# Channel attention with a squared-ReLU feed-forward: the sums of the squares' blocks on GpSimd, and both roundings one step later

## The chip, the cores and the metric

The kernel runs on one core of one Trainium2 chip. The metric is the device time of one execution in microseconds, as a median over runs. The core's engines work in parallel, each through its own instructions in order: TensorE (PE in the profile; PEld are its weight loads) multiplies matrices, ScalarE (ACT) and VectorE (DVE) work elementwise, GpSimd (POOL) too, and SyncE (SP) issues the transfers. They wait for one another through semaphores.

## The reference

```python
# q, k, v: (4, 6080, 256), tau: scalar; w_in: (256, 2048), w_out: (2048, 256), all fp32
qn = q / (norm(q, axis=1) + 1e-6); kn = k / (norm(k, axis=1) + 1e-6)
s = kn.transpose(0, 2, 1) @ qn / tau            # 256 x 256 for each batch
a = softmax(s)
x = (v @ a).reshape(4 * 6080, 256)
h = maximum(x @ w_in, 0)
out = (h * h) @ w_out
```

## The kernel before

**Two products.** The attention matrix of a batch is multiplied into w_in once, to W (256 x 2048), so that for each block of tokens only two products are left: the first, v by W, then ReLU and square, and the second, by w_out. A batch has 12 blocks of tokens, 10 of 512 columns and 2 of 480, in all 48 blocks. fp32 accuracy comes from splitting each operand in a rounded part (`hi`) and a remainder (`lo`) and adding three products: hi by hi, hi by lo, lo by hi.

**Steps.** The loop over `i` at the end of the kernel (line 964) goes through the steps; a step is one of the 16 feature tiles (128 features) of a block. `part` is 0 in an even and 1 in an odd step. Two steps make a pair `(b, n, r)`, 8 pairs make a block. In each step `first_product` (line 712) issues 6 matmuls of 512 columns into PSUM (`ps_h`, 3 buffers) and one eviction with ReLU by ScalarE into half of the pair's tile `x`. The tile has 8 slots of 256 columns; slots 0 to 3 are the four plain blocks (two feature tiles by two halves of the tokens). It lies in a pool with two buffers for this tag.

**Seven products in place of eight.** From the third block on, `by_seven` (line 704) is true, up to the first 5 pairs of the last block: 365 pairs. The second product of a pair is then a 2 x 2 block product done with seven block products (the Strassen-Winograd form): on the side of the squares it needs the plain blocks 1, 2 and 3 and four sums of blocks, in slots 4 to 7. `squares_and_sums` (line 736), in the odd step, has ScalarE square slots 0 to 3, VectorE make the four sums (one subtraction of two slots, one addition, one subtraction), ScalarE round the three plain blocks to `g_hi` (a CAST of 768 columns) and VectorE make their remainder `g_lo`. `parts_of_sums` (line 749), in the next even step, rounds the four sums (1024 columns) and makes their remainder; it is the last reader of `x`. `g_hi` and `g_lo` have two buffers each. The first two blocks use `eight_products`, without sums.

**Order of the work.** Every engine's instructions keep the order in which the program issues them (`InProgramOrder`, line 19). The second product of a pair (`second_product`, line 762) comes two pairs later (`LAG = 2`): in the even step `seven_products` uses plain blocks 1 to 3 (9 matmuls of 256 columns into `ps_o`), in the odd step the four sums (12 matmuls). At the end of a block ScalarE copies the 3 and 4 accumulated blocks to `o`, after the even and the odd part, and `combine` (line 822) adds them up on VectorE, piece by piece in later odd steps, and has SP write them out.

**Work beside it.** While the blocks of one batch run, a generator (`attention`, line 433) issues the attention of the next one piece by piece: in an even step, between the eviction and the work on the pair, one piece of ScalarE and VectorE (in turn the rounding of a chunk of q and k with its remainder, and its squares with their addition), and matmuls into `gram`. Two steps of each block go without. Afterwards the same generator makes the softmax and W. `split_v_hi` and `split_v_lo` round the next block's v at steps 6 and 8 of a block.

Of the kernel before, what the change touches and what calls it, by code (L numbers as in the profile page):

```python
# [30 lines left out]
def kernel(  # L31
# [22 lines left out]
    tensor, vector, scalar, pool_engine = (  # L54
        InProgramOrder(tc, e) for e in (nc.tensor, nc.vector, nc.scalar, nc.gpsimd)
    )
# [624 lines left out]
    def load_v(b, n, tag="v"):  # L681
        t0, tn = blocks[n]
        raw = pool.tile([P, NC, T], F32, tag=tag, name=f"v{b}_{n}", bufs=1)
        nc.sync.dma_start(raw[:, :, :tn], vT[b, :, t0 : t0 + tn].rearrange("(c p) t -> p c t", p=P))
        V[b, n] = [raw, None, None]

    def split_v_hi(b, n):
        tn = blocks[n][1]
        V[b, n][1] = pool.tile([P, NC, T], F32R, tag="v_hi", name=f"v_hi{b}_{n}")
        scalar.copy(V[b, n][1][:, :, :tn], V[b, n][0][:, :, :tn])  # L690
# [5 lines left out]
    def split_v_lo(b, n):  # L696
        tn = blocks[n][1]
        raw, hi, _ = V[b, n]
        V[b, n][2] = pool.tile([P, NC, T], F32R, tag="v_lo", name=f"v_lo{b}_{n}")
        vector.tensor_sub(V[b, n][2][:, :, :tn], raw[:, :, :tn], hi[:, :, :tn].bitcast(F32))  # L700
# [3 lines left out]
    def by_seven(b, n, r):  # L704


        return (0, 1) < (b, n) and ((b, n) != order[-1] or r < SWITCH)

    X = {}
    G = {}  # L710

    def first_product(b, n, f):
        tn = blocks[n][1]
        _, v_hi, v_lo = V[b, n]
        w_hi, w_lo = W[b, f // FPG]
        f0 = (f % FPG) * P
        ps = ps_h.tile([P, T], F32, tag="h", name=f"ps_h{b}_{n}_{f}")
        parts = [(c, x, y) for x, y in ((w_hi, v_hi), (w_hi, v_lo), (w_lo, v_hi)) for c in range(NC)]
        for i, (c, wt, vt) in enumerate(parts):
            tensor.matmul(  # L720
                ps[:, :tn], wt[:, c, f0 : f0 + P], vt[:, c, :tn], start=i == 0, stop=i == len(parts) - 1
            )
        if f % 2 == 0:
            X[b, n, f // 2] = pool.tile([P, 8, tn // 2], F32, tag="x", name=f"x{b}_{n}_{f // 2}")
        x = X[b, n, f // 2].rearrange("p s t -> p (s t)")
        s = slice((f % 2) * tn, (f % 2 + 1) * tn)
        scalar.activation(x[:, s], ps[:, :tn], AF.Relu)
# [3 lines left out]
    def parts_of(b, n, r):  # L731
        half = blocks[n][1] // 2
        shape = [P, 7 if by_seven(b, n, r) else 4, half]
        return [pool.tile(shape, F32R, tag=name, name=f"{name}{b}_{n}_{r}") for name in ("g_hi", "g_lo")]

    def squares_and_sums(b, n, r):

        x = X[b, n, r]
        G[b, n, r] = hi, lo = parts_of(b, n, r)
        scalar.activation(x[:, 0:4, :], x[:, 0:4, :], AF.Square)  # L740
        if by_seven(b, n, r):
            hi_, lo_, src = hi[:, 0:3, :], lo[:, 0:3, :], x[:, 1:4, :]
            vector.tensor_sub(x[:, 4:6, :], x[:, 1:3, :], x[:, 0:1, :].broadcast_to(list(x[:, 1:3, :].shape)))
            scalar.copy(hi_, src)
            vector.tensor_add(x[:, 6, :], x[:, 2, :], x[:, 4, :])
            vector.tensor_sub(x[:, 7, :], x[:, 3, :], x[:, 6, :])
            vector.tensor_sub(lo_, src, hi_.bitcast(F32))

    def parts_of_sums(b, n, r):

        x = X.pop((b, n, r))
        hi, lo = G[b, n, r]
        if by_seven(b, n, r):
            hi, lo, src = hi[:, 3:7, :], lo[:, 3:7, :], x[:, 4:8, :]
        else:
            src = x[:, 0:4, :]
        scalar.copy(hi, src)
        vector.tensor_sub(lo, src, hi.bitcast(F32))
# [3 lines left out]
    def second_product(b, n, r, part):  # L762
        if by_seven(b, n, r):
            seven_products(b, n, r, part)
        elif (b, n) == order[-1]:
            final_products(b, n, r, part)
        else:
            eight_products(b, n, r, part)
# [145 lines left out]
    pairs = [(b, n, f // 2) for b, n, f in steps[::2]]  # L914
# [49 lines left out]
    for i in range(len(steps) + 2 * LAG):  # L964
        part = now["part"] = i % 2
        if i < len(steps):
            b, n, f = steps[i]
            at = b * NB + n
            first_product(b, n, f)
            if n == NB - 1 and f % FPG == FPG - 1:  # L970
                may_write_W.add((b + 1, f // FPG))

        if i >= PAIR:
            gens = (beside,)
        else:
            if i == 1:
                split_v_lo(*order[1])
            for item in stages.get(i, ()):
                weights.stage(item)
            gens = (first,) if i in steps_of_W else ()  # L980
            if i >= 16 and (i >= 24 or part == 0):
                gens += (squares_of_heads if B > 1 and grams[1].raws else sums,)

        if i >= PAIR and steps[min(i, len(steps) - 1)][2] in (2 * LAG - 2, 2 * LAG - 1):
            gens = ()
        if i < PAIR or part == 0:
            for gen in gens:
                next(gen, None)
        if part == 0 and 0 <= i // 2 - 1 < len(pairs):
            parts_of_sums(*pairs[i // 2 - 1])  # L990
        if part == 1 and i // 2 < len(pairs):
            squares_and_sums(*pairs[i // 2])
        if (part or i >= len(steps)) and late_work:
            if next(late_work[0], "end") == "end":
                late_work.pop(0)
        if i == 2 * LAG:
            for _ in heads:
                pass
        if i >= 2 * LAG:
            second_product(*pairs[i // 2 - LAG], part)  # L1000
        if i in steps_of_W:
            next(first)
        if i < len(steps):
            at_hi, at_lo = (None, None) if at == 0 else (12, 13) if at == 1 else (6, 8)
            if i == 2 and len(order) > 2:
                load_v(*order[2])
            if f == at_hi and at + 1 < len(order):
                split_v_hi(*order[at + 1])
            if f == at_lo and at + 1 < len(order):
                split_v_lo(*order[at + 1])  # L1010
                if at + 2 < len(order):
                    load_v(*order[at + 2])
        if i >= PAIR and part:
            for gen in gens:
                next(gen, None)
# [27 lines left out]
```

## Time and profile before

| | |
|---|---|
| median of 2 runs | 2214.74 us (2213.72 to 2215.77) |
| span of the profiled execution | 2211.6 us |
| busy: TensorE, weight loads | 2203.1 us, 1985.0 us |
| busy: VectorE | 1818.0 us, 2614 instructions |
| busy: ScalarE | 1859.1 us, 2347 instructions |
| busy: GpSimd | 0.7 us, 6 instructions |

The times are those of the runs without a profile; the profiled execution's own time is its span, from the first to the last instruction. In the profile's groups all lines are that of a helper (L27), so instructions are told apart by their tiles and sizes: ACT `x<-ps_h` is the eviction, ACT `x<-x` the square, ACT `g_hi<-x` of 768 and 1024 columns the rounding of the plain blocks and of the sums, DVE `g_lo<-x,g_hi` the remainders, DVE `x<-x` the four sums. Pairs of the last two blocks of a batch have 480, 720, 960 and 240 where the others have 512, 768, 1024 and 256. In a row of a timeline the first number is the start and the second the duration, both in us; in brackets stands the engine's idle time before it and what ended it. In a row of windows the busy time and the number of instructions of PE, PEld, DVE, ACT and POOL follow on the window's length, then the granted TensorE clock, the DMA share and GB/s.

### The profile page before, as it was taken

To read this page: it belongs to the slowest core of one execution; us is meant where nothing else is said; L and a number is where in the kernel's file an instruction comes from. 1 tells how busy PE (TensorE), PEld (TensorE's weight loads), DVE (VectorE), ACT (ScalarE), POOL (GpSimd) and SP (SyncE) were. 2 spreads that over 40 slices of the span, in tenths; PEclk is the share of its full clock that TensorE was granted. 3 is DMA by queue.
4 is the path that set the end of the run, shared out by engine and by line. 5 is a ranking of instruction groups with operands and counts; after the bars stand their busy time and mean duration, and the time that the engine had idled before them with its cause. 6 is when DMAs were issued, how large, how long until landed. Compare 5 with 4: busy or idle time off the path is not lost.

```text
span 2211.6 us, 34981 instructions
## 1 busy us (share of the span) xinstructions
PE 2203.1 (100%) x13903; PEld 1985.0 (90%) x13903; DVE 1818.0 (82%) x2614; ACT 1859.1 (84%) x2347; POOL 0.7 (0%) x6
## 2 busy tenths in 40 slices
PE   9999999999999999999999999999999999999999
PEld 8789999988999999998999999999899988888898
DVE  6878888889888888878888888887888877787776
ACT  5788888888888888888878888888888888888887
POOL 0000000000000000000000000000000000000000
PEclk9999999999999999999999999999999999999999
DMA  9521122023421122210122122111103010010000
GB/s 342 179 77 39 61 77 65 27 76 109 157 86 58 60 62 71 63 60 21 36 95 86 60 66 76 58 53 60 33 24 115 22 36 20 22 37 20 20 28 19
DMA packets 82261, 148.03 MB, mean 67 GB/s; under 512 B 8368, under 2 KB 35760, under 8 KB 82096
## 3 DMA queue, kind: packets, MB, share of 16 engines
q1 hardware_dynamic: 82096, 145.79, 19.9%
q8 instruction: 109, 1.79, 0.3%
q14 instruction: 56, 0.46, 0.1%
HBM read 112.46 MB, written 33.29 MB: 66 GB/s over the span
## 4 chain that ended last, share of the span: by engine, by line
PE 92%; DVE 3%; DMA 2%; ACT 2%; issue 0%; SPq 0%; DVEq 0%; ACTq 0%
PE ps_h L27 46%; PE ps_o L27 41%; PE gram L27 4%; PE ps_w L27 2%; DMA qk<-in_k 1%; DVE g_lo L27 1%; DVE x L27 1%; ACT x L27 1%; DMA qk<-in_q 0%; DMA qk_heads<-in_q 0%; ACT g_hi L27 0%; DVE o L27 0%; DMA w_raw<-in_w_in 0%; DVE dec_m L27 0%; DMA wi_lo<-wi_kept 0%
## 5 line engine op out<-in xcount | busy, mean ns | idle before, releaser
L27 DVE TENSOR_TENSOR g_lo<-x,g_hi 128x768 fp32r<-128x768 f32 (+2 forms) x749 | 808.2, 1079 | 71.7 <-ACT g_hi L27 71.1
L27 DVE TENSOR_TENSOR x<-x 128x512 f32<-128x512 f32 (+1 forms) x1095 | 558.2, 510 | 244.0 <-ACT x L27 218.3
L27 ACT CAST g_hi<-x 128x768 fp32r<-128x768 f32 (+2 forms) x749 | 702.1, 937 | 42.8 <-DVE x L27 30.0
L27 ACT ACTIVATE x<-ps_h 128x512 f32<-128x512 f32 (+1 forms) x768 | 456.0, 594 | 248.7 <-PE ps_h L27 228.0
L27 PE MATMUL ps_h<-v_hi,w_hi 128*128 128x512 f32 (+1 forms) x1536 | 478.6, 393 | 0.0
L27 PE MATMUL ps_h<-v_hi,w_lo 128*128 128x512 f32 (+1 forms) x1536 | 477.9, 392 | 0.0
L27 PE MATMUL ps_h<-v_lo,w_hi 128*128 128x512 f32 (+1 forms) x1536 | 474.9, 390 | 0.0
L27 ACT ACTIVATE x<-x 128x1024 f32<-128x1024 f32 (+1 forms) x384 | 404.5, 1053 | 11.9
L27 PE MATMUL ps_o<-g_lo,wS_hi 128*128 128x256 f32 (+1 forms) x1460 | 407.6, 279 | 1.2 <-DVE g_lo L27 1.1
L27 PE MATMUL ps_o<-g_hi,wS_hi 128*128 128x256 f32 (+1 forms) x1460 | 406.1, 278 | 0.8 <-ACT o L27 0.8
L27 PE MATMUL ps_o<-g_hi,wS_lo 128*128 128x256 f32 (+1 forms) x1460 | 406.6, 278 | 0.0
L27 PEld LDWEIGHTS ps_h<-v_lo,w_hi 128*128 128x128 f32 x1536 | 287.9, 187 | 64.9
L27 PEld LDWEIGHTS ps_h<-v_hi,w_lo 128*128 128x128 f32 x1536 | 288.5, 188 | 62.4 <-DVE w_lo L27 0.3
L27 PE MATMUL ps_o<-g_hi,wo_hi 128*128 128x256 f32 (+2 forms) x1159 | 325.2, 285 | 0.6 <-ACT g_hi L27 0.6
L27 PE MATMUL ps_o<-g_hi,wo_lo 128*128 128x256 f32 (+2 forms) x1159 | 325.1, 285 | 0.0
L27 PE MATMUL ps_o<-g_lo,wo_hi 128*128 128x256 f32 (+2 forms) x1159 | 324.8, 285 | 0.1
L27 PEld LDWEIGHTS ps_o<-g_lo,wS_hi 128*128 128x128 f32 x1460 | 274.8, 188 | 17.9 <-DVE g_lo L27 2.1
L27 PEld LDWEIGHTS ps_o<-g_hi,wS_hi 128*128 128x128 f32 x1460 | 274.1, 188 | 17.2 <-ACT o L27 1.6
L27 PEld LDWEIGHTS ps_o<-g_hi,wS_lo 128*128 128x128 f32 x1460 | 274.4, 188 | 0.0
L27 PEld LDWEIGHTS ps_h<-v_hi,w_hi 128*128 128x128 f32 x1536 | 237.4, 188 | 3.6
L27 PEld LDWEIGHTS ps_o<-g_hi,wo_hi 128*128 128x128 f32 x1159 | 218.3, 188 | 15.7 <-ACT g_hi L27 1.0
L27 PEld LDWEIGHTS ps_o<-g_lo,wo_hi 128*128 128x128 f32 x1159 | 217.7, 188 | 15.2 <-DVE g_lo L27 0.5
(120 smaller groups left out, 1776.1 us busy)
## 6 DMA issues: line engine op xcount, KB each, us to landing
qk<-in_k SPq DMA_DIRECT2D x87, 256.0 KB, 2.8
qk<-in_q SPq DMA_DIRECT2D x87, 256.0 KB, 3.0
v<-in_vT SPq DMA_DIRECT2D x40, 512.0 KB, 3.8
out_T<-o SPq DMA_DIRECT2D x152, 128.0 KB, 1.7
wiS<-wi_sums_kept SPq DMA_DIRECT2D x24, 512.0 KB, 5.7
wi_hi<-wi_kept SPq DMA_DIRECT2D x16, 512.0 KB, 4.5
wi_lo<-wi_kept SPq DMA_DIRECT2D x16, 512.0 KB, 3.8
w_raw<-in_w_in SPq DMA_DIRECT2D x4, 1024.0 KB, 6.4
```

The source lines that it names most:

```text
L27: return lambda *args, **kwargs: self.tc.keep_in_program_order(issue(*args, **kwargs))
```

## The change

The three instructions that make the four sums go from VectorE to GpSimd (`pool_engine`), still issued behind the square in the odd step. The rounding of the plain blocks and their remainder move out of `squares_and_sums` into a new function, `parts_of_squares`, which the loop calls one step later, in the even step where `parts_of_sums` was called. `parts_of_sums` moves one step on too, into the next odd step, behind the square of the pair that follows. Pairs that are not done by seven keep their order.

```diff
@@ squares_and_sums
         scalar.activation(x[:, 0:4, :], x[:, 0:4, :], AF.Square)
         if by_seven(b, n, r):
+            pool_engine.tensor_sub(
+                x[:, 4:6, :], x[:, 1:3, :], x[:, 0:1, :].broadcast_to(list(x[:, 1:3, :].shape))
+            )
+            pool_engine.tensor_add(x[:, 6, :], x[:, 2, :], x[:, 4, :])
+            pool_engine.tensor_sub(x[:, 7, :], x[:, 3, :], x[:, 6, :])
+
+    def parts_of_squares(b, n, r):
+
+        if by_seven(b, n, r):
+            x, (hi, lo) = X[b, n, r], G[b, n, r]
             hi_, lo_, src = hi[:, 0:3, :], lo[:, 0:3, :], x[:, 1:4, :]
-            vector.tensor_sub(x[:, 4:6, :], x[:, 1:3, :], x[:, 0:1, :].broadcast_to(list(x[:, 1:3, :].shape)))
             scalar.copy(hi_, src)
-            vector.tensor_add(x[:, 6, :], x[:, 2, :], x[:, 4, :])
-            vector.tensor_sub(x[:, 7, :], x[:, 3, :], x[:, 6, :])
             vector.tensor_sub(lo_, src, hi_.bitcast(F32))
@@ the loop over the steps
         if part == 0 and 0 <= i // 2 - 1 < len(pairs):
-            parts_of_sums(*pairs[i // 2 - 1])
+            pair = pairs[i // 2 - 1]
+            if by_seven(*pair):
+                parts_of_squares(*pair)
+            else:
+                parts_of_sums(*pair)
         if part == 1 and i // 2 < len(pairs):
             squares_and_sums(*pairs[i // 2])
+        if part == 1 and 0 <= i // 2 - 1 < len(pairs) and by_seven(*pairs[i // 2 - 1]):
+            parts_of_sums(*pairs[i // 2 - 1])
```

## The prediction

> **What bounds the kernel now.** I read the page first (busy times and the chain that ended last), then the windows of whole blocks, then the timeline of one pair on each engine.
>
> ```profile
> span 2211.6 us, 34981 instructions
> PE 2203.1 (100%) x13903; PEld 1985.0 (90%) x13903; DVE 1818.0 (82%) x2614; ACT 1859.1 (84%) x2347; POOL 0.7 (0%) x6
> ...
> PE 92%; DVE 3%; DMA 2%; ACT 2%; issue 0%; SPq 0%; DVEq 0%; ACTq 0%
> ```
> ```profile
> 241.10:428.19 187.09, 187.09 (x1221) 169.92 (x1220) 159.45 (x213) 163.13 (x201) 0.00 (x0) 1.00 0.18 57
> 649.53:977.88 328.35, 328.35 (x2139) 297.88 (x2138) 278.67 (x372) 286.31 (x351) 0.00 (x0) 1.00 0.20 62
> 1194.74:1523.09 328.35, 328.35 (x2139) 297.89 (x2138) 278.68 (x372) 286.30 (x351) 0.00 (x0) 1.00 0.20 62
> 1781.79:2116.73 334.94, 334.94 (x2115) 300.80 (x2114) 258.07 (x368) 282.38 (x345) 0.00 (x0) 1.00 0.08 26
> ```
>
> TensorE has 8.5 us without a matmul in the whole span, and in these windows none, at a granted clock of 1.00. It carries the chain. So no change to VectorE, ScalarE or GpSimd can gain more than 8.5 us; the only question is whether it makes TensorE wait. The last window is 8 plain blocks (64 pairs of 33 matmuls): 41.87 us a block, 5.23 us a pair. The other three are 4, 7 and 7 blocks that carry the next batch's attention: 328.35 / 7 = 46.91 us a block, with (2139 - 7 x 264) / 7 = 42 more matmuls each. One pair of the plain stretch:
>
> ```profile
> 1821.17 1.05 ACT L27 CAST g_hi<-x 128x1024 fp32r<-128x1024 f32 x1
> 1823.03 0.60 ACT L27 ACTIVATE x<-ps_h 128x512 f32<-128x512 f32 x1 [0.81 <-PE ps_h L27]
> 1823.66 1.06 ACT L27 ACTIVATE x<-x 128x1024 f32<-128x1024 f32 x1
> 1824.75 0.83 ACT L27 CAST g_hi<-x 128x768 fp32r<-128x768 f32 x1
> 1825.82 0.60 ACT L27 ACTIVATE x<-ps_h 128x512 f32<-128x512 f32 x1 [0.23 <-PE ps_h L27]
> ```
> ```profile
> 1822.25 1.22 DVE L27 TENSOR_TENSOR g_lo<-x,g_hi 128x1024 fp32r<-128x1024 f32 x1 [0.25 <-ACT g_hi L27]
> 1824.75 1.61 DVE L27 TENSOR_TENSOR x<-x 128x512 f32<-128x512 f32 x3 [1.28 <-ACT x L27]
> 1826.28 0.95 DVE L27 TENSOR_TENSOR g_lo<-x,g_hi 128x768 fp32r<-128x768 f32 x1
> ```
>
> ScalarE's order is: odd eviction, square, plain rounding (768), even eviction, sum rounding (1024). Both evictions wait for TensorE: ScalarE has about 1 us a pair to spare, VectorE about 1.5.
>
> **The change: what is removed.**
>
> ```profile
> L27 DVE TENSOR_TENSOR x<-x 128x256 f32<-128x256 f32 x608 | 258.5, 425 | 20.9
> L27 DVE TENSOR_TENSOR x<-x 128x512 f32<-128x512 f32 x304 | 209.9, 690 | 176.2 <-ACT x L27 175.5
> L27 DVE TENSOR_TENSOR x<-x 128x240 f32<-128x240 f32 x122 | 49.8, 408 | 4.2
> L27 DVE TENSOR_TENSOR x<-x 128x480 f32<-128x480 f32 x61 | 40.0, 656 | 42.8 <-ACT x L27 42.8
> ```
>
> VectorE loses 558 us in 304 + 61 = 365 pairs. All of it lies under TensorE's matmuls, so it is worth nothing.
>
> **The change: what is moved.** The plain rounding and its remainder go from the odd step to the next even one, behind the even eviction. They must be there for the pair's second product two steps after that, over 3 us later: free. The sum rounding and its remainder go from the even step to the odd step, behind the next pair's square. TensorE needs the sums one step after the plain blocks, so that deadline alone would still be met. The cost is in the tile x: it has two buffers, the sum remainder is its last reader, and the even eviction of the pair after next takes the buffer again. No moved step issues a DMA, and SP's queue isn't touched. Before, the remainder was done 2.35 us ahead of that eviction (1823.47 to 1825.82 above); now ScalarE's next instruction behind the sum rounding is that very eviction. That the release counts for the whole tile, although the remainder reads slots 4 to 7 and the eviction writes slots 0 and 1, is seen where VectorE was late:
>
> ```profile
> 1236.98 1.22 DVE L27 TENSOR_TENSOR g_lo<-x,g_hi 128x1024 fp32r<-128x1024 f32 x1
> ```
> ```profile
> 1232.66 0.60 ACT L27 ACTIVATE x<-ps_h 128x512 f32<-128x512 f32 x1 [0.96 <-PE ps_h L27]
> 1233.16 1.05 ACT L27 CAST qk_hi<-qk 128x1024 fp32r<-128x1024 f32 x1
> 1234.09 1.06 ACT L27 CAST g_hi<-x 128x1024 fp32r<-128x1024 f32 x1
> ...
> 1238.30 0.60 ACT L27 ACTIVATE x<-ps_h 128x512 f32<-128x512 f32 x1 [0.63 <-DVE g_lo L27]
> ```
> ```profile
> 502.89 0.84 ACT L27 CAST g_hi<-x 128x768 fp32r<-128x768 f32 x1
> 503.63 0.59 ACT L27 ACTIVATE x<-ps_h 128x512 f32<-128x512 f32 x1
> ```
>
> The remainder ends at 1238.20, the eviction begins at 1238.30. So the change closes a loop in every pair, ScalarE to VectorE and back, with ScalarE standing still while VectorE works. Its length, start to start, from the rows above (an instruction that doesn't need the one ahead starts about 0.1 before that one ends: 0.50 behind an eviction, 0.74 behind a plain rounding, 0.95 behind a square): square 0.95, sum rounding 1.05, to VectorE 0.03 (1822.22 to 1822.25), sum remainder 1.22, back 0.10, even eviction 0.50, plain rounding 0.74, odd eviction 0.63. Sum 5.22 us, as long as TensorE's 5.23 by itself. What else ScalarE does in an even step now comes on top, since nothing is left to absorb it:
>
> ```profile
> L27 ACT ACTIVATE qk<-qk 128x1024 f32<-128x1024 f32 x63 | 66.4, 1054 | 0.0
> L27 ACT CAST qk_hi<-qk 128x1024 fp32r<-128x1024 f32 x63 | 65.9, 1045 | 0.0
> L27 ACT CAST v_hi<-v 128x1024 fp32r<-128x1024 f32 x40 | 41.8, 1046 | 0.0
> L27 ACT COPY o<-ps_o 128x768 f32<-128x768 f32 x38 | 30.2, 796 | 0.0
> ```
>
> A block has one v_hi (0.95) and one 768 copy of o (0.70); the 1024 copy is issued in the odd step, behind the sum rounding, and falls into the wait. A plain block: 8 x 5.22 + 1.65 = 43.4 us against 41.87, so +1.54. An attention block has 7 pieces of qk (126 over 18 blocks), each issued in an even step: + 6.65, 50.06 against 46.91, so +3.15. 18 x 3.15 = 57 us; the other 28 of 46 blocks, the stretches that make W among them, counted as plain: 43 us. Together +100 us.
>
> **The change: what is added.** GpSimd gets three instructions a pair behind the square; its queue is otherwise empty. No row shows it at two-input arithmetic. Its nearest rows:
>
> ```profile
> 0.73 0.20 POOL masks.py:197 MEMSET ident<- 128x128 f32 x1 [0.29 <-POOLq L1033]
> 1.01 0.29 POOL masks.py:199 TENSOR_SCALAR_AFFINE_SELECT ident<-ident 128x128 f32<-128x128 f32 x1
> ```
>
> From the second, scaled by size: 1.16 us for 512 columns and 0.58 for 256, 2.32 us a pair; VectorE's rows give 0.69 + 0.43 + 0.43 = 1.55 from below. The sum rounding of that pair comes a whole period later, so the new wait ScalarE for GpSimd costs nothing until GpSimd takes over some 5 us. What it may cost is VectorE: the sum remainder of the pair before is ready 0.95 + 1.05 + 0.03 = 2.03 us after the square's start, while GpSimd reads the other x tile from 1.06 + 0.03 = 1.09 to 2.25. No row shows the two side by side. Bounds: nothing, or all of GpSimd's work, 1.09 + 2.32 + 0.03 - 2.03 = 1.41 us a pair. Nothing in the rows allows a gain. I take the case between, nearer the lower end: VectorE's remainder waits for the first instruction only, 2.28 - 2.03 = 0.25 us, x 365 = 91 us. The Trainium skill, SBUF — State Buffer, section "Who interferes with whom", has this mechanism: a VectorE instruction with two SBUF inputs and a GpSimd instruction that reads SBUF exclude one another, and whichever began first keeps the port for its whole instruction. No run so far shows it. By the GPSIMD Engine Reference, section "Performance versus the Vector engine" (the Trainium skill), an add there takes 1.96 times VectorE's time; an estimate by it is 0.690 x 1.96 = 1.35 us for the first instruction, a wait of 0.44 and 161 us in place of 91, a time of 2476.
>
> Sum: 2211.6 + 100 + 91 = 2402.6 us of span. The median of the runs, 2214.74, lies 3.1 above the span, which gives 2406 us.
>
> **The rivals.** (1) GpSimd and VectorE don't disturb one another: the loop alone, +100, 2315 us. For it: all rows of VectorE were taken without GpSimd, so nothing speaks against. (2) VectorE is kept out until GpSimd is through, or is slowed to half while they overlap, or GpSimd takes so long that the sum rounding waits for it: at the upper end 1.41 x 365 = 515, 2830 us; with half of that about 2570. Against it: GpSimd's second and third instruction each need the one before, which leaves gaps in which VectorE can get in. (3) Not slower: the even eviction isn't held, because only overlapping parts of x count. Then ScalarE's round is 5.22 less 1.40 (the remainder with its hand-overs) and TensorE stays the bound: 2206 to 2215 us. The row at 1238.30 speaks against it. It decides if the loop is 0.2 us a pair shorter than summed, since 8 x 0.2 takes up a plain block's excess. That GpSimd doesn't get the sums at all can't be: the queue is named in the code.
>
> **How the numbers follow.** Forecast 0.47, rival (1) 0.20, (2) 0.23, (3) 0.10. A measurement of this kernel can tell about 2%, 44 us. Forecast, (1) and (2) are all slower by more: 0.90 less 0.01 for a loop somewhat shorter; within 2%: 0.10; faster by over 2% can't come from 8.5 us of idle TensorE: 0.01 for what I overlook. The range leaves out (3) and the upper half of (2): 2300, just under rival (1), to 2750. The forecast's own range, with GpSimd's first instruction between 0.94 us (no wait) and 1.5 us (0.59), is 2315 to 2530.
>
> **What would show it.** The view of who waited for whom has this row, which should grow to about one wait a pair and over 400 us:
>
> ```profile
> ACT x L27 <- DVE g_lo L27: 11.6, 15, 1.5
> ```
>
> TensorE's idle time grows from 8.5 to about 200 us, before ps_o, released by g_lo; a plain block takes 45 to 46 us and an attention block about 52. The 1024 remainder begins when GpSimd's first instruction ends, or shows a longer duration. If it takes 1.22 us and starts 0.03 behind its rounding, rival (1) holds; if it starts behind the third, rival (2). The prediction is wrong if ScalarE's evictions still wait for TensorE alone, or if ScalarE's sum rounding waits for GpSimd.

## The result and the profile after

The changed kernel takes 2437.49 us (2435.48 to 2439.5) against 2214.74: a ratio of 1.1009, 95% interval 1.0977 to 1.1041. It is slower by 10%; 2406 us were forecast, in a range of 2300 to 2750. The span of the profiled execution is 2433.7 us. Of the four executions of `two_halves`, further down, one took 5465.55 us; its time there is the median of the other three.

The page of the changed kernel, busy times and the chain that ended last:

```profile
span 2433.7 us, 35291 instructions
PE 2320.7 (95%) x13903; PEld 1994.8 (82%) x13903; DVE 1571.5 (65%) x1519; ACT 1784.1 (73%) x2347; POOL 1376.1 (57%) x1101
...
ACT 54%; DVE 27%; PE 12%; issue 4%; DMA 1%; ACTq 0%; SPq 0%; DVEq 0%
ACT x L27 25%; DVE g_lo L27 22%; ACT g_hi L27 21%; PE ps_h L27 6%; PE ps_o L27 5%; ACT qk_hi L27 3%; ACT qk L27 2%; ACT v_hi L27 2%; DVE o L27 1%; ACT o L27 1%; PE ps_w L27 1%; DVE v_lo L27 1%; DVE acc L27 1%; DMA qk<-in_k 0%; DVE w_lo L27 
```

TensorE still shows 95% busy, but the chain has left it (92% before, 12% now). It runs through three groups, `x`, `g_hi` and `g_lo`, that is eviction and square, rounding, and remainder: ScalarE and VectorE in turn. With VectorE at 65% and ScalarE at 73% busy, that points to a loop that waits for itself. Who waited for whom, in the same kernel:

```profile
DVE g_lo L27 <- ACT g_hi L27: 672.4, 484, 3.2
ACT x L27 <- DVE g_lo L27: 423.3, 260, 4.6
PEld ps_o L27 <- DVE g_lo L27: 190.6, 364, 2.7
```

VectorE waits for ScalarE's rounding, ScalarE's eviction for VectorE's remainder (11.6 us before, 423.3 now), and TensorE, at the end of the line, for the remainder, once in nearly each of the 365 pairs. The second row counts 260 waits and not 365: in 95 further pairs the eviction behind the sum rounding stands still as long (1.53 us in the mean), but the view puts it down to TensorE's `ps_h`. The timeline of a plain pair, ScalarE, VectorE and GpSimd:

```profile
2010.83 1.06 ACT L27 ACTIVATE x<-x 128x1024 f32<-128x1024 f32 x1
2011.79 1.03 ACT L27 CAST g_hi<-x 128x1024 fp32r<-128x1024 f32 x1
2014.43 0.60 ACT L27 ACTIVATE x<-ps_h 128x512 f32<-128x512 f32 x1 [1.61 <-DVE g_lo L27]
2014.93 0.83 ACT L27 CAST g_hi<-x 128x768 fp32r<-128x768 f32 x1
2015.65 0.60 ACT L27 ACTIVATE x<-ps_h 128x512 f32<-128x512 f32 x1
2016.28 1.06 ACT L27 ACTIVATE x<-x 128x1024 f32<-128x1024 f32 x1
```
```profile
2012.86 1.48 DVE L27 TENSOR_TENSOR g_lo<-x,g_hi 128x1024 fp32r<-128x1024 f32 x1 [1.57 <-ACT g_hi L27]
2015.79 0.96 DVE L27 TENSOR_TENSOR g_lo<-x,g_hi 128x768 fp32r<-128x768 f32 x1 [1.45 <-ACT g_hi L27]
```
```profile
2011.96 1.30 POOL L27 TENSOR_TENSOR x<-x 128x512 f32<-128x512 f32 x1 [1.67 <-ACT x L27]
2013.34 1.59 POOL L27 TENSOR_TENSOR x<-x 128x256 f32<-128x256 f32 x1
2015.01 0.74 POOL L27 TENSOR_TENSOR x<-x 128x256 f32<-128x256 f32 x1
```

From square to square 5.45 us pass, where TensorE needs 5.23. ScalarE stands still for 1.61 us, from the sum rounding to the end of the sum remainder (2014.34) and 0.09 more. The contention is not an idle time of VectorE or GpSimd in any row; it sits in their durations. The remainder takes 1.48 us where it took 1.22, and GpSimd's second instruction 1.59 where the third, of the same size but with VectorE idle, takes 0.74. These are windows of 5 attention blocks and 7 plain blocks of the changed kernel:

```profile
1366.49:1629.91 263.42, 252.07 (x1528) 213.84 (x1527) 170.28 (x147) 198.53 (x250) 151.23 (x120) 1.00 0.18 57
1964.96:2286.28 321.32, 308.71 (x1850) 263.54 (x1849) 182.53 (x155) 231.56 (x301) 210.44 (x168) 1.00 0.08 24
```

That is 52.68 us an attention block (46.91 before) and 45.90 a plain one (41.87 before).

### The profile page after: what moved, and what is told of

It is laid out like the page before. It is cut to its first block, busy times and chain, and to the rows that moved or that the text cites. A ratio compares the mean times of both kernels' runs of the same rounds, so it can differ in the third digit from the quotient of the medians.

```text
span 2433.7 us, 35291 instructions
## 1 busy us (share of the span) xinstructions
PE 2320.7 (95%) x13903; PEld 1994.8 (82%) x13903; DVE 1571.5 (65%) x1519; ACT 1784.1 (73%) x2347; POOL 1376.1 (57%) x1101
## 4 chain that ended last, share of the span: by engine, by line
ACT 54%; DVE 27%; PE 12%; issue 4%; DMA 1%; ACTq 0%; SPq 0%; DVEq 0%
ACT x L27 25%; DVE g_lo L27 22%; ACT g_hi L27 21%; PE ps_h L27 6%; PE ps_o L27 5%; ACT qk_hi L27 3%; ACT qk L27 2%; ACT v_hi L27 2%; DVE o L27 1%; ACT o L27 1%; PE ps_w L27 1%; DVE v_lo L27 1%; DVE acc L27 1%; DMA qk<-in_k 0%; DVE w_lo L27 0%
## 5 line engine op out<-in xcount | busy, mean ns | idle before, releaser
L27 POOL TENSOR_TENSOR x<-x 128x512 f32<-128x512 f32 (+1 forms) x1095 | 1375.4, 1256 | 1035.8 <-ACT x L27 978.6
L27 DVE TENSOR_TENSOR g_lo<-x,g_hi 128x768 fp32r<-128x768 f32 (+2 forms) x749 | 945.8, 1263 | 675.5 <-ACT g_hi L27 672.4
L27 ACT ACTIVATE x<-ps_h 128x512 f32<-128x512 f32 (+1 forms) x768 | 457.5, 596 | 591.3 <-DVE g_lo L27 423.3
L27 ACT CAST g_hi<-x 128x768 fp32r<-128x768 f32 (+2 forms) x749 | 692.5, 925 | 0.0
L27 PE MATMUL ps_o<-g_lo,wS_hi 128*128 128x256 f32 (+1 forms) x1460 | 437.0, 299 | 58.0 <-DVE g_lo L27 56.7
L27 PE MATMUL ps_o<-g_lo,wo_hi 128*128 128x256 f32 (+2 forms) x1159 | 342.4, 300 | 33.0 <-DVE g_lo L27 32.7
```

The source lines that it names most:

```text
L27: return lambda *args, **kwargs: self.tc.keep_in_program_order(issue(*args, **kwargs))
```

## The experiments

Three theories stood at the start. A: the loop through the release of x, as forecast. B: the sums come too late for the second product. C: GpSimd slows VectorE through the port that they share, and this is the main price.

**split_x: the loop is cut.** The four sums go to a tile of their own, so that the sum remainder no longer holds x:

```diff
-            X[b, n, f // 2] = pool.tile([P, 8, tn // 2], F32, tag="x", ...)
+            X[b, n, f // 2] = pool.tile([P, 4, tn // 2], F32, tag="x", ...)
+            y = Y[b, n, r] = pool.tile([P, 4, blocks[n][1] // 2], F32, tag="y", ...)
             pool_engine.tensor_sub(
-                x[:, 4:6, :], x[:, 1:3, :], x[:, 0:1, :]...
+                y[:, 0:2, :], x[:, 1:3, :], x[:, 0:1, :]...
...
-            hi, lo, src = hi[:, 3:7, :], lo[:, 3:7, :], x[:, 4:8, :]
+            hi, lo, src = hi[:, 3:7, :], lo[:, 3:7, :], Y.pop((b, n, r))
```

> The changed kernel, with the tile x cut in two of 4 slots each: x keeps the squares, a new tile y takes the four sums; two buffers each, the same memory. The sum remainder then reads y, and the even eviction takes back x, whose last readers are GpSimd and the plain remainder. Theory A (a loop ScalarE, VectorE, ScalarE through the release of x): TensorE is the bound again, 2205 to 2225 us, 41.9 us a plain block and 47 an attention block; evictions wait for TensorE; the sum remainder still takes 1.48 us, at no cost. Theory B (the sums simply come too late for the second product): nothing of the deadline is changed, 2437 us. Theory C (GpSimd slows VectorE as a whole, through the port they share): nothing of that is changed either, about 2437 us.

Measured: 2292.92 us, 1.0359 (1.0344 to 1.0375). The windows of its attention stretch (7 blocks) and its plain stretch (8 blocks):

```profile
1200.18:1542.32 342.14, 332.69 (x2145) 298.42 (x2144) 265.97 (x216) 279.81 (x358) 230.40 (x168) 1.00 0.21 67
1860.39:2195.57 335.18, 335.18 (x2115) 300.83 (x2114) 231.88 (x177) 270.59 (x344) 272.97 (x193) 1.00 0.08 26
```

In the plain stretch TensorE is the bound again, 41.90 us a block with GpSimd at work all along: there theory A holds alone, and GpSimd's work is as good as free. But an attention block still takes 48.88 us, and the total missed the expected 2205 to 2225 by some 70 us: A isn't all. Where the attention loses is seen around one v remainder, VectorE and GpSimd of the same run:

```profile
1333.20 0.95 DVE L27 TENSOR_TENSOR g_lo<-x,g_hi 128x768 fp32r<-128x768 f32 x1
1334.07 2.31 DVE L27 TENSOR_TENSOR v_lo<-v,v_hi 128x1024 fp32r<-128x1024 f32 x1
1336.30 1.75 DVE L27 TENSOR_TENSOR g_lo<-y,g_hi 128x1024 fp32r<-128x1024 f32 x1
1337.98 1.68 DVE L27 TENSOR_TENSOR o<-o 128x256 f32<-128x256 f32 x2
1339.57 1.22 DVE L27 TENSOR_TENSOR acc<-acc,qk 128x1024 f32<-128x1024 f32 x1
1340.71 2.04 DVE L27 TENSOR_TENSOR g_lo<-x,g_hi 128x768 fp32r<-128x768 f32 x1
```
```profile
1333.61 1.69 POOL L27 TENSOR_TENSOR y<-x 128x512 f32<-128x512 f32 x1 [1.75 <-ACT x L27]
1335.37 3.27 POOL L27 TENSOR_TENSOR y<-x,y 128x256 f32<-128x256 f32 x2
1339.57 2.37 POOL L27 TENSOR_TENSOR y<-x 128x512 f32<-128x512 f32 x1 [0.92 <-ACT x L27]
```

VectorE has no idle time there, yet its rows are long: 2.31 for a remainder that takes 1.22, 2.04 for one of 0.95. Each waits for one of GpSimd's instructions, and GpSimd's for VectorE's in turn. The v remainder ends at 1336.38, which is 1.22 behind 1335.16, shortly before the end of GpSimd's first instruction at 1335.30.

**before_split: a control.** The kernel before with the same cut and the sums on VectorE.

> The kernel before with x and y cut apart as in the run named split_x, sums on VectorE: a control of the cut itself. Theory A and its rivals alike: 2205 to 2216 us, the 15 waits of evictions for g_lo gone.

Measured: 2213.35 us, 1.0001 (0.9992 to 1.001). The cut itself costs nothing, and the evictions' waits for `g_lo` are gone, as expected.

**sums_on_vector: the loop without GpSimd.** The order of the changed kernel, with the three instructions issued to VectorE, behind the sum remainder of the pair before:

```diff
+        if part == 1 and i // 2 < len(pairs):
+            sums_of_squares(*pairs[i // 2])   # the three instructions, on vector
```

> The changed kernel's order, with the sums made by VectorE, behind the sum remainder of the pair before; GpSimd does nothing. Theory A: the loop stays, without the wait for GpSimd: 365 x 0.26 us and some 45 x 0.54 us (a v remainder that holds GpSimd up, and it the sum remainder) less than 2437, so 2318 us (2300 to 2340); the remainder of 1024 takes 1.22 us. Theory B: sums are ready sooner, so about 2215. Theory C: all of the loss goes, about 2215 us.

Measured: 2332.76 us, 1.054 (1.0525 to 1.0556). Its timeline, ScalarE and VectorE:

```profile
2060.68 1.06 ACT L27 ACTIVATE x<-x 128x1024 f32<-128x1024 f32 x1
2061.64 1.03 ACT L27 CAST g_hi<-x 128x1024 fp32r<-128x1024 f32 x1
2064.03 0.60 ACT L27 ACTIVATE x<-ps_h 128x512 f32<-128x512 f32 x1 [1.35 <-DVE g_lo L27]
...
2065.87 1.06 ACT L27 ACTIVATE x<-x 128x1024 f32<-128x1024 f32 x1
```
```profile
2062.70 1.23 DVE L27 TENSOR_TENSOR g_lo<-x,g_hi 128x1024 fp32r<-128x1024 f32 x1 [1.57 <-ACT g_hi L27]
```

The loop is 5.19 us, the remainder takes 1.23, and ScalarE waits 1.35 us for it. The total lies in the range that was expected for theory A. So GpSimd isn't needed for a loss of 5%, 118 of the 223 us (2332.76 and 2437.49 less 2214.74), which rules C out as the main cause, though the other 105 us go with GpSimd. This run doesn't rule B out: the sums are ready sooner, but their rounding keeps its late place, and with it the deadline. What speaks against B as the main cause is `split_x`, which left that place as it was and whose plain blocks lose nothing; the next two runs give B its size.

**split_on_vector: neither the loop nor GpSimd.** Both edits together.

> The order of the changed kernel, x cut in x and y as in split_x, and the sums on VectorE behind the sum remainder of the pair before as in sums_on_vector: neither the loop nor GpSimd is left. With the runs so far (changed kernel 2437, GpSimd without the loop 2293, the loop without GpSimd 2333) it completes a square of four. If these two are all, TensorE is the bound: 2205 to 2222 us, 41.9 and 47 us a block. If something else in the later roundings costs (a deadline, the order on ScalarE), it stays above: 2240 us or more.

Measured: 2240.21 us, 1.012 (1.0106 to 1.0134). Plain blocks take 41.87 us, but 26 us are left in the attention blocks and the stretches that make W. TensorE's waits before the second product name the remainder there: its weight loads waited 27 times, 17.6 us in all, for `g_lo`.

**sums_in_time: what these 26 us are.** In that kernel the sum rounding goes back to the even step; the plain rounding stays late.

```diff
                 parts_of_squares(*pair)
-            else:
-                parts_of_sums(*pair)
+            parts_of_sums(*pair)
         ...
-        if part == 1 and 0 <= i // 2 - 1 < len(pairs) and by_seven(*pairs[i // 2 - 1]):
-            parts_of_sums(*pairs[i // 2 - 1])
```

> The run split_on_vector (2240 us) with the rounding of the sums and its remainder back in the even step, behind the plain rounding; the plain rounding stays one step later. If what is left of split_on_vector's excess of 26 us is the deadline of the sums (one step less until the second product's odd half), the time is that of the kernel before, 2210 to 2220 us. If it is the plain rounding's place behind the eviction, or VectorE's order, it stays at 2235 us or more.

Measured: 2214.87 us, 1.0008 (0.9999 to 1.0017). TensorE's weight loads wait 4.5 us for `g_lo` in place of 17.6. So the 26 us are the deadline of the sums (theory B, as a small term); the plain rounding's move is free.

**The square.** Four times, in us, all with the later roundings:

| | sums on VectorE | sums on GpSimd |
|---|---|---|
| x cut in two: no loop | 2240 | 2293 |
| x whole: loop | 2333 | 2437 |

The later roundings alone cost 26, the loop 93 without GpSimd and 145 with it, GpSimd 53 without the loop and 105 with it. Beside these runs the kernel before took between 2213.1 and 2214.7 us, so the differences hold to some 2 us.

**engine_only: the other half of the change alone.** The kernel before with the three instructions issued to GpSimd, nothing moved.

> The kernel before with one edit: the four sums are issued to GpSimd; the roundings stay where they were. Theory A (GpSimd takes 3.8 us a pair beside VectorE): the sum rounding in the even step waits for GpSimd and holds the odd eviction behind it; a round of ScalarE is square 1.06, hand-over 0.07, GpSimd about 3.5, rounding 0.95, eviction 0.63, some 6.2 us against 5.23: 2540 to 2640 us, ScalarE's g_hi waits for POOL once a pair. Rival: 3.8 us fit into a period of 5.23, and the move of the roundings was what cost: 2215 us.

Measured: 2641.92 us, 1.1937 (1.1917 to 1.1957), 2 us above the expected range. This is ScalarE in that run:

```profile
2106.09 1.06 ACT L27 ACTIVATE x<-x 128x1024 f32<-128x1024 f32 x1
...
2110.78 1.05 ACT L27 CAST g_hi<-x 128x1024 fp32r<-128x1024 f32 x1 [2.27 <-POOL x L27]
2111.73 0.59 ACT L27 ACTIVATE x<-ps_h 128x512 f32<-128x512 f32 x1
2112.36 1.06 ACT L27 ACTIVATE x<-x 128x1024 f32<-128x1024 f32 x1
```

A round takes 6.27 us: the sum rounding waits for GpSimd and holds the evictions behind it. Without a later sum rounding GpSimd's latency lies on ScalarE's path; with it, the release of x does.

**v_lo_later and v_lo_13: the missing 31 us.** In the changed kernel, the remainder of v at step 9, then at step 13, in place of step 8.

```diff
-            at_hi, at_lo = (None, None) if at == 0 else (12, 13) if at == 1 else (6, 8)
+            at_hi, at_lo = (None, None) if at == 0 else (12, 13) if at == 1 else (6, 9)    # v_lo_later
+            at_hi, at_lo = (None, None) if at == 0 else (12, 13) if at == 1 else (6, 13)   # v_lo_13
```

What led to them is one pair of each block in the changed kernel, VectorE and GpSimd:

```profile
1999.98 1.21 DVE L27 TENSOR_TENSOR v_lo<-v,v_hi 128x1024 fp32r<-128x1024 f32 x1
2001.41 2.02 DVE L27 TENSOR_TENSOR g_lo<-x,g_hi 128x1024 fp32r<-128x1024 f32 x1 [0.22 <-ACT g_hi L27]
```
```profile
2000.52 1.82 POOL L27 TENSOR_TENSOR x<-x 128x512 f32<-128x512 f32 x1 [1.61 <-ACT x L27]
```

The v remainder has room on VectorE, but it is still running when GpSimd's first instruction wants to read: that takes 1.82 us in place of 1.30, and the sum remainder behind it 2.02 in place of 1.48.

> The changed kernel with the remainder of v (and the load behind it) issued one step later, at the end of step 9 of a block in place of step 8, behind the sum remainder and not ahead of it. Theory A with an exclusive port: once a block the v remainder holds GpSimd's first instruction and that the sum remainder (2.02 us in place of 1.48); without it a plain block takes 45.3 us in place of 45.86, in all some 45 x 0.54 = 24 us less, 2413 us. Rival (the v remainder has nothing to do with the excess over the predicted 2406): 2437 us.

Measured: 2458.65 us, 1.1108 (1.1092 to 1.1125): slower by 21, not faster by 24. At step 9 the v remainder comes right ahead of the plain remainder, and GpSimd's first instruction waits for both, and the sum remainder for that:

```profile
2026.28 2.09 POOL L27 TENSOR_TENSOR x<-x 128x512 f32<-128x512 f32 x1 [1.61 <-ACT x L27]
```
```profile
2027.16 2.28 DVE L27 TENSOR_TENSOR g_lo<-x,g_hi 128x1024 fp32r<-128x1024 f32 x1
```

That pair takes 6.25 us from square to square, where it took 5.99: the crowd had only moved.

> The changed kernel with the remainder of v issued at the end of step 13 of a block in place of step 8: behind the sum remainder, where VectorE then has about 1.45 us before the plain remainder, and in a pair without the adding up of the block before. Theory (one pair of a block, that with the remainder of v, takes 5.99 us in place of 5.46, since v's remainder holds GpSimd's first instruction up and that the sum remainder): every pair takes 5.46, 45 x 0.53 = 24 us less, 2413 us. Rival (where it stands doesn't matter, VectorE and GpSimd just have that much more to do in one port): 2430 to 2460 us, as at step 9 with 2459.

Measured: 2419.08 us, 1.0925 (1.091 to 1.094): 18 less, where the theory had 24; between the profiled executions it is 22. From square to square a plain block takes 45.34 us in place of 45.86, as the theory has it.

**split_v_lo_13: the same in split_x.**

> The run split_x with the remainder of v at step 13. There the plain blocks take 41.9 us, and the attention blocks 48.6 and 49.5 in turn, against 46.95 before. Theory P (one crowded place: v's remainder, the adding up of the block before and a piece of q and k within three pairs, all against GpSimd): spread out, the attention blocks come near 47.3, 18 x 1.7 = 31 us less, about 2262 us. Theory Q (VectorE's and GpSimd's claims on the port fill an attention block on the whole): no change, 2285 to 2295 us.

Measured: 2267.03 us, 1.024 (1.0226 to 1.0254): 26 less than `split_x`, near the 31 of theory P, and half of what GpSimd costs without the loop. Seven attention blocks take 332.1 us from square to square, hardly more than in `split_on_vector` without GpSimd (331.3) and 10.4 less than in `split_x` (342.5). So the port isn't full there; single crowded places cost. Most of what is left of GpSimd's price lies in the stretches that make W.

**two_halves: who keeps the port, and how long.** GpSimd's first instruction cut in two.

```diff
-            pool_engine.tensor_sub(
-                x[:, 4:6, :], x[:, 1:3, :], x[:, 0:1, :].broadcast_to(list(x[:, 1:3, :].shape))
-            )
+            for i in (0, 1):
+                pool_engine.tensor_sub(x[:, 4 + i, :], x[:, 1 + i, :], x[:, 0, :])
```

> The changed kernel with GpSimd's first instruction (512 columns) cut in two of 256. Exclusive port, who comes first keeps it for its whole instruction: the sum remainder is ready 2.03 us after the square's start, the first half is through at about 1.9, the second then begins ahead of the remainder and holds it to about 2.55: 1.74 us in place of 1.48, 365 x 0.26 = 95 us more, 2530 us. Rival (both run side by side, each slowed in proportion to the overlap): no change, 2425 to 2450 us. If the remainder gets in between the halves instead: 1.22 us, about 2340.

Measured: 2448.63 us, 1.1064 (1.1042 to 1.1086), 11 more than the changed kernel. The time is that of the rival, but the rows speak for the exclusive port. GpSimd's two halves together, and the remainder behind them:

```profile
2046.93 1.44 POOL L27 TENSOR_TENSOR x<-x 128x256 f32<-128x256 f32 x2 [1.67 <-ACT x L27]
```
```profile
2047.83 1.63 DVE L27 TENSOR_TENSOR g_lo<-x,g_hi 128x1024 fp32r<-128x1024 f32 x1 [1.57 <-ACT g_hi L27]
```

The first half (0.74) is through before the remainder is ready; the second has begun, and the remainder waits for it, 1.63 us where it took 1.48. The second half isn't slowed by the remainder beside it, as it would be by the rival: the two take 1.44 with a small overlap, 0.74 and 0.75. They end 2.57 us behind the square's start (2045.80), close to the expected 2.55. Two other things were wrong in the expectation. It compared 1.74, counted from GpSimd's reported end, with a measured 1.48, in which VectorE gets in some 0.14 before that end; so a usual pair takes 5.60 us in place of 5.46, and not 0.26 more. And it left out the pair with the v remainder:

```profile
2013.20 2.94 POOL L27 TENSOR_TENSOR x<-x 128x256 f32<-128x256 f32 x2 [1.61 <-ACT x L27]
```
```profile
2014.09 1.47 DVE L27 TENSOR_TENSOR g_lo<-x,g_hi 128x1024 fp32r<-128x1024 f32 x1 [0.21 <-ACT g_hi L27]
```

There the sum remainder is ready while the first half holds the port, and goes ahead of the second half, whose row begins at 2014.43: it takes 1.47 us where it took 2.02. This pair takes 5.44 us in place of 5.99 and the next one 5.20 in place of 5.46, so that a plain block comes to 45.89 against 45.86. That the total hardly moved is two effects that cancel.

## Why the prediction was right, and where not

**Right: the bound and the loop.** It was right that nothing could be gained from VectorE's 558 us, that the release of x counts for the whole tile, and that a loop of 5.22 us arises: it measured 5.19 without GpSimd. About one wait a pair for the remainder and over 400 us were forecast; the row shows 423.3 us in 260 waits, and the other pairs' waits stand under TensorE's name. The chance given to "slower by over 2%" was 0.89.

**Right in the sum, by luck, since two errors cancel: the wait for GpSimd.** The forecast was 0.25 us a pair, and 1.48 - 1.22 = 0.26 was measured. But GpSimd's first instruction took 1.30 us, not 1.16, and began 0.07 behind the square, not 0.03; that alone would have made it 0.43. In return VectorE was let in before GpSimd's reported end (2013.26): counted back from its own end, 2014.34 - 1.22 = 2013.12, some 0.14 earlier, and the hand-over of 0.03 wasn't due. The Trainium skill, SBUF — State Buffer, section "Who interferes with whom", had the mechanism, and the trace agrees: who began first kept the port for its whole instruction, in both directions (1.48 on VectorE, 1.59 on GpSimd), to within that 0.14 us. The GPSIMD Engine Reference, section "Performance versus the Vector engine" (the Trainium skill), has a ratio of 1.96; measured here were 1.30 against 0.69, a ratio of 1.88, and 0.74 against 0.425, 1.74.

**Mis-sized: the two sums by block.** 2406 was 31 us too low. One missing term is the v remainder, which was counted at nothing: it has room on VectorE, but holds GpSimd up, which holds the loop up. It measured 18 us between the medians, 22 between the profiled executions. The other is in "the stretches that make W among them, counted as plain". With the v remainder out of the way (`v_lo_13`) a plain block takes 45.34 us and an attention block 52.03, against 43.41 + 8 x 0.25 = 45.41 and 50.06 + 2.0 = 52.06 by the prediction. But the 15 blocks between the attention stretches, in which W is made, take 63 us more than before, against 15 x (1.54 + 2.0) = 53; that is the rest, since this run's span, 2411.9, lies 9 above the summed 2402.6. GpSimd isn't needed for it: in `sums_on_vector`, where it is idle, they take 36 us more, against 15 x 1.54 = 23. The sums' deadline could be what is missing, since it alone costs 18 us in these blocks; no run parts it from the loop there, so this stays open.

**Wrong: "that deadline alone would still be met".** The sums' deadline isn't met everywhere: it costs 25 us (`split_on_vector` against `sums_in_time`), 18 of them in the stretches that make W, some 5 in the attention, none in the plain blocks. In the attention blocks it doesn't come on top of the loop, by the 52.03 us above. That the plain roundings move for free was right.

**Off: TensorE's idle time.** About 200 us were forecast, 113 are shown (2433.7 - 2320.7). The busy time of PE rose by 117.6 us with the same 13903 matmuls, so part of the waiting seems to be counted into their rows; the share of PEld, 90% to 82%, shows the loss better.

**The rivals.** (1), no contention, asked for 2315 us; the nearest run, `sums_on_vector`, took 2333, and in the changed kernel the remainder took 1.48 us and not 1.22. (2) and (3) didn't come about: VectorE gets in behind the first instruction, and the eviction is held.

No version among these beats the kernel before, which had 8.5 us of TensorE to gain.

## What to carry to other kernels

Before work is moved a step later, ask which buffer its last read holds, and who takes that buffer next: where that is the very next instruction of the engine that also feeds the reader, a loop closes, and two engines run in turn though neither is full. Work moved to GpSimd to relieve VectorE isn't out of its way: in these runs, instructions with two SBUF inputs on both excluded one another (1.22 us became 1.48), and the wait was found in longer durations, not in idle times. It was free only where no such instruction of VectorE was on the critical path (41.90 us a plain block in `split_x`). Count for each such instruction, on either engine, which one it may be standing in front of.

## What the runs showed of the hardware that was not expected

The blocked instruction gets in some 0.14 us before the reported end of the other, counted back from its own end, in both directions: VectorE's at 2013.12 with GpSimd's row to 2013.26, and GpSimd's at 2014.93 - 0.74 = 2014.19 with VectorE's row to 2014.34. An engine that is kept from the port passes the delay on: a 1.21 us remainder with room of its own cost the pair 0.53 us by way of GpSimd. A sum remainder that already waited (from 2014.09) went ahead of GpSimd's independent second half (from 2014.43) in `two_halves`, so it waited for one instruction and not for both. GpSimd isn't sure of the same: in `engine_only` an instruction of 480 columns that takes 1.23 us otherwise took 3.65 (at 683.88), while three of VectorE's went ahead. What decides between the two isn't shown. Two independent GpSimd instructions of 256 columns took 1.44 us together, where each alone has 0.74 and one of 512 columns takes 1.30.
